# First batch of a cross-attention and feed-forward kernel: the second matrix mixed amid group 0's products, w_out pieces ordered behind w_in's, and a quarter of the products held back

## The chip, the cores and the metric

The kernel runs on one core of a Trainium2 chip. The metric is device microseconds of one launch. A change counts as faster or slower beyond 2%. Engines: PE (TensorE, matrix products), ACT (ScalarE), DVE (VectorE), SP (which issues most transfers).

## The reference

```python
# x: (8, 8, 512, 64), state: (8, 8, 32, 64); per batch and head
a     = softmax(scale * x @ state.T);  xread = a @ state
a2    = softmax(scale * state @ x.T);  sread = a2 @ x
rows  = concat([xread, sread])         # -> (8 * 544, 512)
h     = rows @ w_in                    # (512, 2048)
g     = h * erf(softplus(h))
out   = g @ w_out                      # (2048, 512)
```

Both weight matrices come as 64-bit floats and are turned into 32-bit on the chip, by bit operations.

## The kernel before

The weights come in sixteen pieces of 1 MB, eight of w_in and eight of w_out, two of each per group of 512 hidden columns. A piece lands in one of three raw buffers. Two instructions of ACT and three of DVE (L113, L114, L115 in the profile) convert it; then its raw buffer is free for the next transfer.

```python
raw = act.tile([P, 2 * shape[0] * i], U32, name="raw", bufs=3)
fetched.append(nc.sync.dma_start(out=raw..., in_=src.bitcast(U32)))
...
nc.scalar.activation(out=dst, in_=hi.bitcast(F32), func=ACTF.Copy, scale=2.0 ** -112)   # L111
nc.scalar.activation(out=lo, in_=lo, func=ACTF.Copy, scale=2.0 ** -29)                  # L112
nc.vector.tensor_scalar(d, d, 3, None, op0=ALU.logical_shift_left)                      # L113
nc.vector.tensor_tensor(d, d, lo, op=ALU.add)                                           # L114
nc.vector.scalar_tensor_tensor(out=d, in0=hi, scalar=0x80000000, in1=d, ...)            # L115
```

For each group of the first batch, `mixed` multiplies w_in by the state and copies the result out as the matrix m (L253 on PE, L255: one half copied by ACT, the other by DVE). `hidden` makes h in four banks (two in PSUM at a time; each is read by softplus on ACT, L272, and by a copy, L273). `finish` is one erf on ACT (L276) and one multiply on DVE (L277). `project` multiplies by w_out into four accumulators, here called blocks (L283).

```python
gT, hs, finish, banks = hidden(0, range(GF), 0, S, nc.scalar.copy)
...
at = finish()
acc = tiles(NC)
project(gT, 0, acc)
for g in range(1, NG):
    for j in range(2):
        behind(banks[j][:2] if g > 1 else at, weights_in, 2 * g + j)
    at, = mixed(0, g)
    for j in range(2):
        behind(at, weights_out, 2 * g + j)
    ...
    before, (gT, hs, finish, banks) = gT, hidden(0, range(GF * g, GF * g + GF), 0, S)
    at = finish()
    if g > 1:
        project(before, g - 1, acc)
```

`behind(marks, f, ...)` orders the instructions of f behind the marks in their engines' queues. The order in a queue is fixed when the program is built.

## Time and profile before

| what | before |
|---|---|
| time, median of 3 | 819.48 us |
| profiled run | 820.32 us, span 818.5 us |
| PE busy | 795.4 us, 97% of the span |
| PE waits between 36 and 82 us | 10.7 us in four waits |
| first w_out product | 38.82 us |
| third h bank of group 2 starts | 84.02 us |

The last two rows are milestones. The third bank of group 2 is where the stretch that the change touches ends; after it PE runs with hardly a gap (busy 726.1 of the 731.0 us from 84.02 to 815).

### The profile page before, as it was taken

To read this page: it belongs to the slowest core of one execution; us is meant where nothing else is said; L and a number is where in the kernel's file an instruction comes from. 1 tells how busy PE (TensorE), PEld (TensorE's weight loads), DVE (VectorE), ACT (ScalarE), POOL (GpSimd) and SP (SyncE) were. 2 spreads that over 40 slices of the span, in tenths; PEclk is the share of its full clock that TensorE was granted. 3 is DMA by queue.
4 is the path that set the end of the run, shared out by engine and by line. 5 is a ranking of instruction groups with operands and counts; after the bars stand their busy time and mean duration, and the time that the engine had idled before them with its cause. 6 is when DMAs were issued, how large, how long until landed. Compare 5 with 4: busy or idle time off the path is not lost.

```text
span 818.5 us, 10638 instructions
## 1 busy us (share of the span) xinstructions
PE 795.4 (97%) x4532; PEld 612.8 (75%) x4532; DVE 426.5 (52%) x622; ACT 370.0 (45%) x468; POOL 0.7 (0%) x6
## 2 busy tenths in 40 slices
PE   8887999999999999999999999999999999999997
PEld 7532444588888788878888788878887888888886
DVE  3748784458445554557453744555454745343431
ACT  5837554537333733345343733363334533333220
POOL 0000000000000000000000000000000000000000
PEclk9997999999999999999999999999999999999999
DMA  6636703201100030002000020000000000000000
GB/s 209 206 109 210 217 1 91 65 1 29 49 1 26 1 78 1 27 1 78 1 27 1 18 61 1 26 1 27 1 26 1 27 1 26 1 26 1 26 1 26
DMA packets 47414, 35.27 MB, mean 43 GB/s; under 512 B 36872, under 2 KB 36872, under 8 KB 47368
## 3 DMA queue, kind: packets, MB, share of 16 engines
q1 hardware_dynamic: 45256, 34.09, 13.4%
q10 hardware_dynamic: 2112, 0.52, 0.3%
q8 instruction: 35, 0.57, 0.3%
q14 instruction: 11, 0.09, 0.0%
HBM read 25.69 MB, written 8.91 MB: 42 GB/s over the span
## 4 chain that ended last, share of the span: by engine, by line
PE 86%; ACT 2%; DVE 1%; issue 1%
PE o L335 45%; PE h L270 28%; PE o L283 5%; PE at L253 4%; PE at L156 1%; PE at L214 1%; PE at L226 1%; PE at L179 1%; PE at L197 1%; ACT L272 1%; DVE s L277 1%; ACT s L272 0%; ACT xT L158 0%; ACT sc L170 0%; PE at L166 0%
## 5 line engine op out<-in xcount | busy, mean ns | idle before, releaser
L270 PE MATMUL h<-aT,m 128*128 128x256 f32 (+1 forms) x960 | 242.9, 400 | 3.9 <-DVE hs L273 3.1
L270 PEld LDWEIGHTS h<-aT,m 128*128 128x128 f32 x960 | 178.6, 191 | 68.1 <-issue 33.0
L273 DVE COPY hs<-h 128x512 f32<-128x512 f32 x132 | 90.7, 690 | 186.4 <-ACT s L272 186.2
L272 ACT ACTIVATE s<-h 128x512 f32<-128x512 f32 x136 | 80.3, 597 | 160.4 <-PE h L270 159.8
L277 DVE TENSOR_TENSOR s<-s,hs 128x2048 f32<-128x2048 f32 x34 | 77.9, 2292 | 76.0 <-ACT s L276 75.9
L335 PE MATMUL o<-w_out,s 128*128 128x256 f32 x480 | 114.9, 380 | 1.6 <-DVE s L277 1.6
L335 PE MATMUL o<-raw,hs 128*128 128x256 f32 x480 | 115.6, 380 | 0.0
L335 PE MATMUL o<-w_out,hs 128*128 128x256 f32 x480 | 113.4, 379 | 0.0
L335 PEld LDWEIGHTS o<-w_out,s 128*128 128x128 f32 x480 | 90.2, 190 | 14.3 <-DVE s L277 2.5
L335 PEld LDWEIGHTS o<-w_out,hs 128*128 128x128 f32 x480 | 91.1, 190 | 12.4
L335 PEld LDWEIGHTS o<-raw,hs 128*128 128x128 f32 x480 | 90.3, 190 | 12.4
L255 ACT COPY m<-at 128x512 f32<-128x512 f32 (+1 forms) x33 | 18.9, 573 | 165.4 <-PE at L253 165.3
L276 ACT ACTIVATE s<-s 128x2048 f32<-128x2048 f32 x34 | 64.9, 1910 | 0.4
L283 PE MATMUL o<-w_out,s 128*128 128x512 f32 x128 | 59.7, 607 | 1.8 <-DVE s L277 1.7
L335 PE MATMUL o<-raw,s 128*128 128x256 f32 x240 | 56.7, 379 | 0.0
L255 DVE COPY m<-at 128x512 f32<-128x512 f32 (+1 forms) x33 | 22.3, 675 | 60.0 <-PE at L253 60.0
L272 ACT ACT_TABLE_LOAD x40 | 51.3, 1283 | 0.7
L335 PEld LDWEIGHTS o<-raw,s 128*128 128x128 f32 x240 | 45.2, 190 | 5.9
L283 PEld LDWEIGHTS o<-w_out,s 128*128 128x128 f32 x128 | 23.4, 192 | 33.1 <-issue 29.2
L276 ACT ACT_TABLE_LOAD x34 | 43.6, 1283 | 0.6
L253 PE MATMUL at<-w_in,stT 64*32 64x512 f32 (+1 forms) x528 | 38.0, 602 | 5.6 <-DVE w_in L115 5.2
L346 ACT COPY m<-o 128x256 f32<-128x256 f32 x15 | 5.6, 373 | 57.3 <-PE o L335 57.3
(72 smaller groups left out, 584.8 us busy)
## 6 DMA issues: line engine op xcount, KB each, us to landing
raw<-in_moe_w_in_dram SPq DMA_DIRECT2D x8, 1024.0 KB, 5.3
raw<-in_moe_w_out_dram SPq DMA_DIRECT2D x8, 1024.0 KB, 4.9
out_dram<-ot SPq DMA_DIRECT2D x32, 256.0 KB, 2.4
x<-in_x_dram SPq DMA_DIRECT2D x60, 128.0 KB, 2.7
x<-in_x_dram ACTq DMA_DIRECT2D x4, 128.0 KB, 3.4
out_dram<-ot SPq DMA_DIRECT2D x8, 64.0 KB, 1.7
st<-in_state_dram SPq DMA_DIRECT2D x8, 56.0 KB, 4.4
st<-in_state_dram SPq DMA_DIRECT2D x2, 32.0 KB
```

The source lines that it names most:

```text
L156: nc.tensor.transpose(out=xp[:, P * c:P * c + P], in_=xt[:, c, 2 * i:2 * i + 2, :], identity=ident)
L179: on_pe = nc.tensor.transpose(out=s1[:, NI * c:NI * c + NI, :], in_=sc[:, e, P * c:P * c + P], identity=ident)
L197: nc.tensor.transpose(out=ps[:, P * c:P * c + P], in_=a[:, e, NI * c:NI * c + NI, :], identity=ident)
L253: nc.tensor.matmul(out=ps[e][q, :], lhsT=stT[b][r, q], rhs=w_in[r, fs, i, :], start=True, stop=True)
L255: return nc.scalar.copy(mg[:, 0], ps[0]), nc.vector.tensor_copy(mg[:, 1], ps[1])
L270: on_pe = nc.tensor.matmul(out=hp[:, n * j:n * j + n], lhsT=lhsT, rhs=rhs, start=(k == 0), stop=(k == len(ops) - 1))
L272: banks.append((nc.scalar.activation(out=s[:, i, :], in_=hp, func=ACTF.Softplus), copy(hs[:, i, :], hp), on_pe))
L273: copy(hs[:, i, :], hp), on_pe))
L276: return (nc.scalar.activation(out=s, in_=s, func=ACTF.Erf), nc.vector.tensor_tensor(s, s, hs, op=ALU.mult))
L277: nc.vector.tensor_tensor(s, s, hs, op=ALU.mult))
L283: nc.tensor.matmul(out=acc[r], lhsT=gT[:, i, P * r:P * r + P], rhs=w_out[:, GF * g + i, :], start=(g == 0 and i == 0), stop=(g == NG - 1 a ...
L335: nc.tensor.matmul(out=acc[bank][:, E2 * c:E2 * c + E2], lhsT=lhs[:, i, :], rhs=rhs[:, g, i, :], start=(first and i == 0 and c == 0), stop ...
```

## The change

Intent: (a) of group 0's four bank copies, two go to DVE, so that erf starts sooner. (b) The second matrix is mixed after two of the four blocks of group 0. (c) w_out piece 2 is converted directly behind the w_in pieces, in a stretch where ACT was idle, and w_in 4 directly behind w_out 3. (d) Block 3 is held back: three of its products run between the hidden banks of group 1, the last one after the third mixing.

```diff
-    gT, hs, finish, banks = hidden(0, range(GF), 0, S, nc.scalar.copy)
+    gT, hs, finish, banks = hidden(0, range(GF), 0, S,
+                                   [nc.scalar.copy] * 2 + [nc.vector.tensor_copy] * 2)
...
-    project(gT, 0, acc)
     for g in range(1, NG):
-        for j in range(2):
-            behind(banks[j][:2] if g > 1 else at, weights_in, 2 * g + j)
-        at, = mixed(0, g)
-        for j in range(2):
-            behind(at, weights_out, 2 * g + j)
+        if g == 1:
+            for j in range(2):
+                made = behind(at, weights_in, 2 + j)
+            project(gT, 0, acc, range(2))
+            at, = mixed(0, 1)
+            behind([made], weights_out, 2)
+            made = behind(at, weights_out, 3)
+            project(gT, 0, acc, range(2, 3))
+        else:
+            if g == 2:
+                behind([made], weights_in, 4)
+                behind(banks[1][:2], weights_in, 5)
+                project(gT_, 0, acc, range(3, 4), range(GF - 1))
+            else:
+                for j in range(2):
+                    behind(banks[j][:2], weights_in, 2 * g + j)
+            at, = mixed(0, g)
+            if g == 2:
+                project(gT_, 0, acc, range(3, 4), range(GF - 1, GF))
+            for j in range(2):
+                behind(at, weights_out, 2 * g + j)
```

(The converting function returns its last instruction, and `project` takes ranges of blocks and products.)

More of the change, by code (lines that the diff above doesn't have):

```diff
@@ L114, in weight @@
         nc.vector.tensor_tensor(d, d, lo, op=ALU.add)
-        nc.vector.scalar_tensor_tensor(out=d, in0=hi, scalar=0x80000000, in1=d,
-                                       op0=ALU.bitwise_and, op1=ALU.bitwise_or)
+        return nc.vector.scalar_tensor_tensor(out=d, in0=hi, scalar=0x80000000, in1=d,
+                                              op0=ALU.bitwise_and, op1=ALU.bitwise_or)
     gw = GF * P
     def weights_in(j):
-        weight(w_in[:, j],
-               moe_w_in[:, 2 * P * j:2 * P * j + 2 * P].rearrange("(k p) f -> p k f", p=P),
-               (NK, 2 * P))
+        return weight(w_in[:, j],
+                      moe_w_in[:, 2 * P * j:2 * P * j + 2 * P].rearrange("(k p) f -> p k f", p=P),
+                      (NK, 2 * P))
     def weights_out(j):
-        weight(w_out[:, 2 * j:2 * j + 2, :],
-               moe_w_out[2 * P * j:2 * P * j + 2 * P].rearrange("(t p) e -> p t e", p=P),
-               (2, d_model))
+        return weight(w_out[:, 2 * j:2 * j + 2, :],
+                      moe_w_out[2 * P * j:2 * P * j + 2 * P].rearrange("(t p) e -> p t e", p=P),
+                      (2, d_model))
     spare = ps_o.tile([P, d_model], F32, name="o3")
@@ L255, in mixed_part, with hidden @@
         return nc.scalar.copy(mg[:, 0], ps[0]), nc.vector.tensor_copy(mg[:, 1], ps[1])
-    def hidden(b, fts, t0, n, copy=nc.vector.tensor_copy):
+    def hidden(b, fts, t0, n, copies=(nc.vector.tensor_copy,) * 4):
         hs = act.tile([P, 4, S], F32, name="hs")
@@ L272, in hidden @@
             banks.append((nc.scalar.activation(out=s[:, i, :], in_=hp, func=ACTF.Softplus),
-                          copy(hs[:, i, :], hp), on_pe))
+                          copies[i](hs[:, i, :], hp), on_pe))
         def finish():
@@ L278, in hidden, with project @@
         return s, hs, finish, banks
-    def project(gT, g, acc):
-        for r in range(NC):
-            for i in range(GF):
+    def project(gT, g, acc, rs=range(NC), ts=range(GF)):
+        for r in rs:
+            for i in ts:
                 nc.tensor.matmul(out=acc[r], lhsT=gT[:, i, P * r:P * r + P],
@@ L430 @@
             states(1)
-        before, (gT, hs, finish, banks) = gT, hidden(0, range(GF * g, GF * g + GF), 0, S)
+        gT_, (gT, hs, finish, banks) = gT, hidden(0, range(GF * g, GF * g + GF), 0, S)
         at = finish()
@@ L435 @@
         if g > 1:
-            project(before, g - 1, acc)
+            project(gT_, g - 1, acc)
     last = combine_w()
```

## The prediction

> **What bounds the kernel now.** I read the page first: busy time by engine, the 40 slices, and the chain that ended last.
>
> ```profile
> PE 795.4 (97%) x4532; PEld 612.8 (75%) x4532; DVE 426.5 (52%) x622; ACT 370.0 (45%) x468; POOL 0.7 (0%) x6
> ...
> PE   8887999999999999999999999999999999999997
> ...
> PEclk9997999999999999999999999999999999999999
> ...
> PE 86%; ACT 2%; DVE 1%; issue 1%
> ```
>
> The chain is matrix products (PE) for 86% of the span. The only slices with a visible hole are the first four (20.5 us each), and in the fourth the clock falls too. After that PE is the bound, so a microsecond saved early should arrive unchanged at the end. The change touches only the first batch, so I went to the list of waits of PE between 36 and 82 us.
>
> ```profile
> PE at L253 <- DVE w_in L115: 5.2, 1, 5.2
> PE h L270 <- DVE hs L273: 3.1, 1, 3.1
> PE o L283 <- DVE s L277: 1.7, 1, 1.7
> PE h L270 <- ACT m L255: 0.7, 1, 0.7
> ```
>
> Columns: who waited for whom, total us, times, longest. Then PE alone in order of time over the same stretch (start, length, what, idle before):
>
> ```profile
> 52.75 1.09 PE L253 MATMUL at<-w_in,stT 64*32 64x512 f32 x16
> 54.57 3.70 PE L270 MATMUL h<-aT,m 128*128 128x512 f32 x8 [0.73 <-ACT m L255]
> 61.39 5.36 PE L270 MATMUL h<-aT,m 128*128 128x512 f32 x8 [3.12 <-DVE hs L273]
> 71.91 1.96 PE L253 MATMUL at<-w_in,stT 64*32 64x512 f32 x16 [5.15 <-DVE w_in L115]
> ```
>
> Eight records took 3.70 us in the second row and 5.36 in the third; sixteen took 1.09, then 1.96. The table of one-microsecond stretches says why (the clock is the third number from the right):
>
> ```profile
> 61.00:62.00 1.00, 0.61 (x1) 0.50 (x2) 1.00 (x2) 1.00 (x2) 0.00 (x0) 0.68 0.89 188
> 64.00:65.00 1.00, 1.00 (x3) 0.46 (x2) 1.00 (x1) 0.00 (x0) 0.00 (x0) 0.62 0.95 356
> 71.00:72.00 1.00, 0.10 (x8) 0.13 (x16) 1.00 (x2) 0.63 (x1) 0.00 (x0) 0.80 0.80 328
> 78.00:79.00 1.00, 1.00 (x3) 0.32 (x2) 1.00 (x2) 0.98 (x2) 0.00 (x0) 0.79 0.00 0
> ```
>
> The clock fell to half at about 61.36, rose at 64.75, fell at 71.6, rose at 78.4. So two waits cost 8.3 us, and each cost more afterwards through a slow clock. ACT in order of time shows the cause of both:
>
> ```profile
> 54.41 1.13 ACT L111 ACTIVATE w_out<-raw 128x1024 f32<-128x1024 f32 x1
> ...
> 57.52 1.17 ACT L112 ACTIVATE raw<-raw 128x1024 uint32<-128x1024 uint32 x1
> 58.70 1.28 ACT L272 ACT_TABLE_LOAD   x1
> 60.00 1.08 ACT L272 ACTIVATE s<-h 128x512 f32<-128x512 f32 x2
> ```
>
> Between 40.6 and 53.9 ACT did nothing; at 54.4 it began converting two w_out pieces, just when PE filled its two h banks, and only then evicted them.
>
> [...] 61.36 to 64.75 is 3.4 us, 71.6 to 78.4 is two of them. And the fall at 61.36 came after only 3.1 us of complete idleness. [...] A 128x512 product stands as two records, start to start 0.43 us: 0.857 us per product. [...] the reload before softplus is a fixed 1.28 us. [...] here a piece lands a median 5.2 us after issue (4.8 at the least), and that is what I use.
>
> **The change, part by part.** Arithmetic, bytes and number of products stay. Order moves. I compared the instruction order of the two builds and placed the new order in time with durations of the trace. Steps start to start: conversion on ACT 1.03 per half; on DVE L113 0.60 (0.81 if the next reads it), L114 and L115 1.14 (1.26 if the next reads it); bank copy or softplus 0.6.
>
> (a) Bank copies 2 and 3 of group 0 go from ACT to DVE. ACT has two copies between its softpluses; now the second softplus waits for its product (ends 31.75) and ends 32.40, so the table load starts at 32.41 instead of 33.23: 0.83 earlier. DVE is free: copies at 32.5 and 33.1, the delayed L115 ends at 34.9, before the multiply, due at 35.64 (36.47 before). First w_out product 38.82 -> 37.99. Gain 0.83.
>
> (b) Second matrix amid the products. PE does two of four blocks (8 x 0.857 = 6.86): 44.85. w_in pieces 2 and 3 are converted at 43.99 (44.83 less the 0.83), so mixing runs 45.1 to 46.2 without a wait. Block 2 (3.43) covers the copy of m, until 49.55: the 0.73 wait goes. Four products of hidden fill both h banks until 52.98; three of the kept four run until 55.55.
>
> (c) w_out pieces behind w_in's. Piece 2, issued about 35.0, lands near 41, and is converted by 47.2, in ACT's old hole. Piece 3 needs a raw buffer (three exist), free when DVE finishes the first w_in piece at 42.85; issued 42.9, lands about 47.8. ACT converts it 47.8 to 50.0, then w_in 4 (issued 44.05, landed near 50.1) until 52.3; table load until 53.6, softplus of both banks until 54.8. DVE: piece 3 until 52.5, w_in 4 52.4 to 55.7, bank copies done 56.3 and 56.9. So PE waits 55.55 to 56.40: 0.85 in place of 3.12, and does four products until 59.83.
>
> (d) w_in 5 takes the buffer of w_out 2: issued 47.25, landed by 53, converted on DVE 56.8 to 60.1. PE mixes at 60.27: a wait of 0.45 in place of 5.15, until 61.36; the last kept product runs to 62.15.
>
> (e) A new wait. The copy of m on ACT stands behind softplus of bank 3 (60.5), table load (61.8) and erf (63.7), so it ends at 64.2, and PE has nothing else: 2.1 us idle. Then four products to 67.7, five of group 1 to 72.0, and the third h bank starts.
>
> That last point was at 84.02 before, is now 71.97: 12.05 us earlier. Check by sums: before, from the end of block 3 at 52.5 to 84.02 is 31.5 us; its work is two mixings (2.04), 12 hidden products (10.28) and five others (4.29), 16.6 us. So 14.9 were lost: 9.0 in three waits, the rest by slow clock and changeovers. After, 0.85 + 0.45 + 2.1 + about 0.5 of changeovers, 3.9, remain. 14.9 - 3.9 + 0.83 = 11.8, near the 12.05.
>
> Do the later pieces follow? w_in 6 is issued near 60, w_in 7 near 69.7 and lands by 75. Its conversion ends near 82, and PE wants it at 84.8. w_out 4 and 5 lie between, converted by 72.5, and are wanted at the same time. So nothing eats the gain, by a margin of about 3 us.
>
> **The rivals.** First, the 2.1 us hole of (e) chills the clock. The stretch around it has mixing (small tiles) and one product in it; a mostly idle window sufficed at 58 to 61.4. For it: [...] mixing may count little, as the clock stayed half through 71.9 to 75. Against: 37.1 to 38.8 was idle 1.7 us with no fall, and here the worst window still holds some 1.3 us of work. It would cost one window, about 1.7 us, or two, 3.4: 809 to 811. I give it 15 to 20%. Second, the conversions are the bound: with PE's waits small, the path from 47.8 runs through landing, ACT and DVE. Each microsecond that piece 3 or w_in 4 lands late moves everything after it. For it: both are in flight at once, as in 45 to 51 us before, and share the engines. It makes 808 to 809. Third, the gain is given back later because weights arrive no earlier (waits at third mixing): the margin above speaks against it; it would leave 5 to 8 us of gain, 811 to 814. Fourth, better than thought: earlier landings or no wait for erf, 805.5.
>
> **Range and chances.** 819.5 less 12 gives 807.5. Low 805.5: the 2.1 and the two small waits halved. High 811: a chilled clock, or late pieces. Faster by over 2% needs 16.4 us, but all that was lost is 14.9, and (a) adds 0.83: 15.7. That nearly rules it out: 1%. Slower would need a new stall of over 28 us: 1%.
>
> **What would show each step.** (a) first w_out product near 38.0. (b) mixing at about 45, with no wait at its hidden products. (c) a wait of 0.5 to 2 us at the third h bank, on DVE's copy. (d) under 1 us before the mixing of the third matrix. (e) about 2 us before the next hidden products, on ACT's m. Clock at full rate from 55 to 80. Third h bank of group 2 near 72 instead of 84, and the same distance to the end of the kernel. Wrong: a clock of half after 62, the wait at the third bank above 3 us, or a wait on w_in in the fourth group.

The steps and lengths are from the profile of the kernel before: records of a 128x512 product 0.43 us apart, two per product; the table load 1.283 us (each of the 40 at L272, so "fixed"); landings of 4.8 to 9.7 us, in the median 5.2 (`--tile raw`, 0 to 110 us). The half clock of "one window, about 1.7 us" is the 3.41 us from 61.36 to 64.77. That two pieces in flight share the engines is read off the stretch from 45 to 51 us: the 16 DMA engines were busy for 93% of it and moved 2.07 MB, 345 GB/s.

## The result, and the profile after

The changed kernel took 810.41 us (median of four, 808.74 to 812.89); the kernel before, beside it, 819.72. The ratio is 0.9886, with an interval of 0.9855 to 0.9916. That is 9.3 us less, inside the predicted range of 805.5 to 811, and 2.9 us more than the predicted 807.5. By the 2% rule above the verdict is "same", for this kernel and for all twelve of the experiments; the intervals show that all but `copies_only` are below the kernel before all the same.

The profiled run was the slowest of the four, 812.89 us (above the predicted range). Three lines of its page:

```profile
PE 792.5 (98%) x4532; PEld 611.7 (75%) x4532; DVE 427.9 (53%) x624; ACT 369.3 (46%) x466; POOL 0.7 (0%) x6
...
PEclk9999999999999999999999999999999999999999
...
PE 88%; ACT 3%; DVE 1%; DMA 1%; issue 1%; SPq 0%
```

The 7 in the fourth slice of the clock row is gone. In the chain that ended last, DMA now has 1%: a transfer has come onto the path, where the chain before showed none (nor does that of `again`, below). PE's waits between 36 and 82 us:

```profile
PE h L270 <- DVE hs L273: 2.5, 1, 2.5
PE h L270 <- ACT m L255: 2.0, 1, 2.0
PE o L283 <- DVE s L277: 0.9, 1, 0.9
PE at L253 <- DVE w_in L115: 0.2, 1, 0.2
```

The sum fell from 10.7 to 5.6 us. The wait on the w_in conversion went from 5.2 to 0.2. A new one of 2.0 on ACT's copy of m is what step (e) of the prediction named, and is called the hole from here on. PE in order of time (start, length, what, idle before):

```profile
58.76 3.70 PE L270 MATMUL h<-aT,m 128*128 128x512 f32 x8 [2.55 <-DVE hs L273]
62.71 1.09 PE L253 MATMUL at<-w_in,stT 64*32 64x512 f32 x16 [0.25 <-DVE w_in L115]
66.85 5.40 PE L270 MATMUL h<-aT,m 128*128 128x512 f32 x8 [1.98 <-ACT m L255]
```

The first and the third row are eight records of the same kind, once 3.70 and once 5.40 us. The one-microsecond stretches show the clock (third number from the right):

```profile
67.00:68.00 1.00, 1.00 (x2) 0.48 (x3) 1.00 (x1) 1.00 (x2) 0.00 (x0) 0.59 0.15 55
...
70.00:71.00 1.00, 1.00 (x3) 0.53 (x2) 1.00 (x2) 0.98 (x2) 0.00 (x0) 0.70 0.00 0
```

It fell to half near 67.2 and rose near 70.6, 3.41 us later, which cost 1.7. Before, it was at half from 61.36 to 64.77 and from 71.60 to 78.43, three times as long. The chain of waits tells where the 2.55 came from (start, length, what):

```profile
44.52 8.87 DMA raw<-in_moe_w_in_dram
...
54.44 1.16 ACT raw L112
...
55.62 1.24 DVE w_in L114
...
56.88 1.22 DVE w_in L115
58.11 0.61 DVE hs L273
```

Piece w_in 4 was 8.9 us on its way; its conversion stands ahead of the bank copies on DVE, so the bank copies waited for it.

The third h bank of group 2 starts at 76.37 instead of 84.02: 7.65 us earlier, and the span is 7.7 us shorter (810.8 against 818.5). So the gain is whole at that milestone and nothing after it gives any back. That holds in the other traces too: from the milestone to the end it is 734.4 to 734.8 us in both kernels and in those runs whose PE order from there on is theirs. (In `w_out_late`, `m_on_dve` and `early_m_dve` one product fewer of 0.86 us lies ahead of the milestone and one more behind it: 735.3 us.)

The table places the changed kernel's two profiles (the second is from the experiment `again`) against the prediction, counted from the first w_out product, which sits at 37.8 to 39.5 us depending on how the head of the run (its first 30 us or so) went.

| from the first w_out product, us | predicted | first profile | second profile |
|---|---|---|---|
| third bank of group 1 | 18.41 | 20.34 | 18.38 |
| third mixing | 22.28 | 24.29 | 22.29 |
| hidden products of group 2 | 26.26 | 28.43 | 26.47 |
| third bank of group 2 | 33.98 | 37.95 | 35.99 |

(Predicted: 56.40, 60.27, 64.25 and 71.97 less 37.99. Before, the last row was 84.02 - 38.82 = 45.20.)

### The profile page after: what moved, and what is told of

Same layout as the page of the kernel before. It is cut to its first block, busy times and chain, and to the rows that moved or that the text cites. A ratio compares the mean times of both kernels' runs of the same rounds, so it can differ in the third digit from the quotient of the medians.

```text
span 810.8 us, 10642 instructions
## 1 busy us (share of the span) xinstructions
PE 792.5 (98%) x4532; PEld 611.7 (75%) x4532; DVE 427.9 (53%) x624; ACT 369.3 (46%) x466; POOL 0.7 (0%) x6
## 4 chain that ended last, share of the span: by engine, by line
PE 88%; ACT 3%; DVE 1%; DMA 1%; issue 1%; SPq 0%
PE o L335 45%; PE h L270 29%; PE o L283 5%; PE at L253 4%; PE at L156 1%; DMA raw<-in_moe_w_in_dram 1%; PE at L214 1%; PE at L226 1%; PE at L179 1%; PE at L197 1%; ACT L272 1%; ACT s L276 0%; ACT s L272 0%; ACT L276 0%; ACT xT L158 0%
## 5 line engine op out<-in xcount | busy, mean ns | idle before, releaser
L272 ACT ACTIVATE s<-h 128x512 f32<-128x512 f32 x136 | 80.2, 597 | 160.5 <-PE h L270 159.9
```

What stands on the lines that cost most here:

```text
L272: banks.append((nc.scalar.activation(out=s[:, i, :], in_=hp, func=ACTF.Softplus), copies[i](hs[:, i, :], hp), on_pe))
```

## The experiments

Twelve kernels, each timed over five rounds beside the kernel before. All but the first undo or isolate a part of the change, or take away one suspected cost. All gave correct results. Runs of one call share a chip and the runs of the kernel before.

### again

The changed kernel unaltered.

> The changed kernel unaltered, for its own spread and a second profile. Theory A (the chain runs from the landing of weight piece w_in 4 through ACT, DVE and the third h bank to the erf and the copy of m): the landing was late because the next piece was in flight beside it, so it is late again: wait at the third bank 2 to 3 us, a hole of about 2 us before the third matrix's hidden products, time near 810. Rival B (the late landing was chance): landing about 6 us after issue, wait near 0.9, time near 808. The clock falls to half after the hole in some profiles and not in others[...].

Measured: 810.91 us (809.01 to 812.55), ratio 0.989 (0.9872 to 0.9907). Its PE rows at the same three places:

```profile
56.57 3.70 PE L270 MATMUL h<-aT,m 128*128 128x512 f32 x8 [0.60 <-DVE hs L273]
60.48 1.09 PE L253 MATMUL at<-w_in,stT 64*32 64x512 f32 x16 [0.20 <-DVE w_in L115]
64.66 5.40 PE L270 MATMUL h<-aT,m 128*128 128x512 f32 x8 [2.03 <-ACT m L255]
```

The wait at the third bank was 0.60, and w_in 4 was converted 6.3 us after its issue (44.27 to 50.55). The same two transfers were under way, so the late landing of the first profile was chance (its cause stays open): rival B was right on the mechanism, theory A wrong. But the time did not fall to B's 808: the clock fell to half in the hole here too. Over the nine runs of the two sets, the mean clock was 0.999 or 1.0 in two (808.74 and 809.01 us) and 0.998 or less in seven (810.26 us or more in each, on average 811.2). A stretch of 3.41 us at half clock lowers the mean by 3.41 x 0.5 / 810 = 0.002. The mean alone proves no fall in the hole, for it also counts the end of the run, where PE is done and the clock drops (the kernel before is at half from 815.7 us to its last instruction at 818.5, with PE idle; the profile of `hole_warm` is at half from 806.1 us on, falls nowhere else, and has 0.999). But with the gap in the times, 1.25 us, it makes a fall in the hole likely in those seven, and three of the four profiles of this order with an empty hole show it.

### copies_only

```diff
-    gT, hs, finish, banks = hidden(0, range(GF), 0, S, nc.scalar.copy)
+    gT, hs, finish, banks = hidden(0, range(GF), 0, S,
+                                   [nc.scalar.copy] * 2 + [nc.vector.tensor_copy] * 2)
```

(on the kernel before)

> The kernel before with part (a) alone: bank copies 2 and 3 of group 0 on DVE. If the erf's early start is worth its full length: first w_out product 0.8 us earlier, the rest shifted with it, time 0.8 us under before. Rival: the w_out conversion on DVE, now 1.3 us later, frees its raw buffer later and gives it back: same time as before.

Measured: 819.69 us, ratio 1.0002 (0.9988 to 1.0016). In the trace, from the start of the 24 warming products to the first w_out product it is 6.40 us (32.65 to 39.05), against 7.22 before (31.60 to 38.82): the 0.82 is there locally. At the third bank of group 2 only 0.4 of it is left (52.03 us from the warming products, against 52.42). In the time it does not show; 0.8 us is 0.1%, and lies within the interval.

### copies_back

The same edit reversed, on the changed kernel.

> The changed kernel with part (a) taken back (all four copies on ACT). Theory A: the erf starts 0.8 us later, the transfers that wait for the DVE conversions behind it are issued 0.8 us later: time 0.8 us above the changed kernel. Rival: the path from 44 us on starts with transfers, whose landing absorbs it: within 0.3 us.

Measured: 809.89 us (809.19 to 810.94), ratio 0.988 (0.9866 to 0.9894): no slower than the changed kernel. Locally it lost the same: 7.24 us to the first w_out product. From the two, part (a) is worth at most about 1 us, and the times cannot tell 0.8 from nothing. The profile is worth more for another reason. Its hole is as long as in `again`, 2.04 us, and the eight records took 3.70:

```profile
64.82 3.70 PE L270 MATMUL h<-aT,m 128*128 128x512 f32 x8 [2.04 <-ACT m L255]
```

The same hole with and without a fall: its length alone did not decide whether the clock fell. The traces show what went with the falls. All changes of the clock in one trace lie whole multiples of 3.41 us apart (in the kernel before the stretches between them are 54.61, 3.41, 6.83, 6.83 and 737.28 us, so 16, 1, 2, 2 and 216 times 3.413), on a grid that lies elsewhere in each run (the falls in the hole came at 67.18 in the first profile, 64.96 in `again` and 64.6 in `w_in5_later`); so I counted PE's busy time in each window of the grid. First the window that ended in the fall of the changed kernel, then the one of `copies_back` that holds most of the hole (window, length, PE busy; the clock is third from the right):

```profile
63.77:67.18 3.41, 1.43 (x8) 0.56 (x4) 1.57 (x3) 3.40 (x4) 0.00 (x0) 1.00 0.89 298
...
63.37:66.79 3.42, 1.97 (x5) 1.01 (x6) 2.46 (x2) 3.42 (x5) 0.00 (x0) 1.00 0.50 195
```

In the first the hole lies in one window, of which PE was busy 42%; in the second a border at 63.37 divides it, and the windows held 77% and 58%. Between 36 and 82 us of all fourteen traces, each of the eleven windows that ended in a fall held at most 1.54 us of PE work (45%, `w_in5_later`), and each full-speed window that did not held at least 1.59 (47%, the changed kernel from 56.94 us). The clock came back after a window at half clock of which PE was busy 93% or more, and stayed down after 87% or less; six of the eleven falls lasted one window, four lasted two and one three (`copies_only`, 69.3 to 79.5). The busy times are modelled, so these figures are rough, and they are those of these fourteen traces.

With no fall, the third bank of group 2 stands 34.20 us behind the first w_out product, against 33.98 predicted; but without part (a) that product itself comes 0.84 us later. In `hole_warm`, next, which has part (a) and no fall, it is 34.48.

### hole_warm

```diff
             hp = ps_h.tile([P, S], F32, name="h")
+            if i == 0 and b == 0 and fts[0] == 2 * GF:
+                for _ in range(8):
+                    nc.tensor.matmul(out=hp[:, 0:P], lhsT=ident, rhs=ident, start=True, stop=True)
```

> The changed kernel with 8 idle 128x128 products with the identity put into the hole, in the free h bank that the next product overwrites. They do no work and take no engine that anything waits for. Theory A: the hole stays (the hidden products still start at the copy of m), but the clock does not fall, and the eight records take 3.7 us instead of 5.4: about 1.7 us under the changed kernel in runs where that one's clock fell, and less spread. Rival: the fall has another cause, and the records take 5.4 again.

Measured: 809.09 us (808.53 to 809.90), ratio 0.9863 (0.9843 to 0.9882). The mean clock was 0.999 or 1.0 in all four runs (in 3 of the 13 runs of the changed kernel in `again`, `w_in5_later` and the result).

```profile
63.66 1.95 PE L269 MATMUL h<-ident 128*128 128x128 f32 x16
65.82 3.70 PE L273 MATMUL h<-aT,m 128*128 128x512 f32 x8 [0.21 <-ACT m L255]
```

Idle work of 1.95 us in the hole (here 16 records, two per product) and the next records take 3.70. The hole stays as long; only the clock is kept. Against the two unaltered kernels that is 1.3 to 1.8 us less, and against `w_in5_later` (below, in effect unaltered, same chip) 1.25. The cause of the slow records after this hole is thereby shown: it is PE's idleness in it (3.70 us with the idle products, 5.32 to 5.40 in three of the four profiles without). The times alone would not show it, for the two intervals overlap.

### m_on_dve

```diff
-        return nc.scalar.copy(mg[:, 0], ps[0]), nc.vector.tensor_copy(mg[:, 1], ps[1])
+        copy = nc.vector.tensor_copy if (b, g) == (0, 2) else nc.scalar.copy
+        return copy(mg[:, 0], ps[0]), nc.vector.tensor_copy(mg[:, 1], ps[1])
```

> The changed kernel with both copies of m of the third matrix on DVE, so that none stands behind softplus, table load and erf on ACT. Theory A: the hole shrinks from 2.0 to about 0.6 us and the clock stays: 1.4 plus 1.7 us, so about 3 us under a changed kernel whose clock fell, near 807. Rival: the DVE copy delays the multiply and the conversions behind it, and the wait returns one group later: same time.

Measured: 808.60 us (808.48 to 809.00), ratio 0.9857 (0.9838 to 0.9875).

```profile
62.62 3.70 PE L271 MATMUL h<-aT,m 128*128 128x512 f32 x8
67.84 3.70 PE L284 MATMUL o<-w_out,s 128*128 128x512 f32 x8 [1.52 <-DVE s L278]
```

The hole is gone and the clock stayed up, as theory A has it. But a wait of 1.52 us came after, on DVE's multiply of group 1, which is the rival's point. So the saving was about the clock's 1.7, not 3 us. By the medians, and with a narrow spread, this is the best of all kernels run: 1.7 us under `w_in5_later`, and 1.4% under the kernel before. Its lead of 0.5 us on `hole_warm` and `early_m_dve` is not clear of noise.

### none_kept

```diff
-            project(gT, 0, acc, range(2, 3))
+            project(gT, 0, acc, range(2, 4))
```

(and the two held-back calls removed)

> The changed kernel with no products kept back: block 3 of group 0 runs whole before the hidden products of group 1. Theory A (PE is not the bound between 46 and 67 us): the third h bank starts where it did (near 58.8), with a wait of about 2 us in place of 2.5; the hole before the third matrix's hidden products grows from 2.0 to about 2.9 us, they start where they did, and the clock falls more surely; time within 1 us of the changed kernel. Rival D (the kept quarter hides waits): up to 3.4 us slower.

Measured: 810.78 us, ratio 0.9883 (0.9859 to 0.9906): as the changed kernel. Its PE rows:

```profile
62.98 1.09 PE L253 MATMUL at<-w_in,stT 64*32 64x512 f32 x16 [2.34 <-DVE w_in L115]
65.02 5.29 PE L270 MATMUL h<-aT,m 128*128 128x512 f32 x8 [0.95 <-ACT m L255]
```

There is no wait at the third bank at all; the waiting stands before the third mixing instead. I had the places of the waits wrong (2 us at the bank and 2.9 in the hole were expected). But the sum is about the same (3.3 us, in `again` 2.8), because PE only moves its idle time about: the hidden products of group 2 start 26.54 us after the first w_out product, in `again` 26.47. Part (d) is worth nothing here that the times show.

### w_out_late

```diff
-            behind([made], weights_out, 2)
+            behind(at, weights_out, 2)
```

> The changed kernel with w_out piece 2 ordered behind the copy of m again, as before (part (c) taken back). Theory A (transfers and conversions in sum set the pace, whichever comes first): piece w_in 5 is issued some 4 us later, so w_in 4 lands alone, near 50 us, the wait at the third bank falls under 1 us, and the third mixing starts within 1 us of where it was; time within 1 us of the changed kernel. Rival C (filling ACT's hole is the gain): 3 to 5 us slower than the changed kernel.

Measured: 812.16 us (811.46 to 812.69), ratio 0.9906 (0.9893 to 0.992): 1.3 to 1.8 us slower than the changed kernel, more than the 1 us that theory A allowed and less than rival C's 3 to 5 (the intervals of the two ratios overlap, so that this rests on the medians and on the trace). The wait at the third bank is gone, but piece w_in 5 came later and the whole wait stands before the third mixing:

```profile
63.53 1.96 PE L253 MATMUL at<-w_in,stT 64*32 64x512 f32 x16 [3.30 <-DVE w_in L115]
```

The sixteen records take 1.96: after a wait of 3.3 us in one piece the clock was down, and it stayed at half from 63.44 to 70.24 in this profile, two windows. The first w_out product is 37.16 us before the third bank of group 2, 1.2 more than in `again`; with one product fewer in between, like for like 2.0 more.

### only_amid

The kernel before with part (b), built from the changed kernel by taking (a), (d) and the order of w_out 2 back. One order of (c) stayed: w_in 4 stands behind w_out 3. So this is not (b) alone, as the expectation has it.

```diff
+            project(gT, 0, acc, range(2))
+            at, = mixed(0, 1)
+            behind(at, weights_out, 2)
+            made = behind(at, weights_out, 3)
+            project(gT, 0, acc, range(2, 4))
```

> The kernel before with part (b) alone: second matrix mixed after two of the four blocks of group 0; copies on ACT, w_out pieces behind the copy of m, nothing kept. Theory A': the loss of before was ACT idle until the copy of m at 54 us, with both w_out conversions behind it; mixing at 46 brings that copy, and so the conversions, 7 us forward all by itself. Third mixing near 63.5 as with the w_out pieces late; time within 1.5 us of that run, 811 to 813, most of the gain. Rival (the parts add up): about a third of the gain, 816.

Measured: 814.59 us (813.30 to 815.07), ratio 0.9925 (0.9912 to 0.9937). Two of PE's rows:

```profile
59.56 3.70 PE L270 MATMUL h<-aT,m 128*128 128x512 f32 x8 [1.53 <-DVE hs L273]
...
67.65 6.77 PE L270 MATMUL h<-aT,m 128*128 128x512 f32 x8 [2.37 <-ACT m L255]
```

### not_amid

Parts (a) and (c) without (b) and (d): PE's order is that of before.

```diff
+            project(gT, 0, acc)
+            behind([made], weights_out, 2)
+            at, = mixed(0, 1)
+            made = behind(at, weights_out, 3)
```

> Parts (a) and (c) without (b) and without kept products: PE's order as before, w_out piece 2 behind the w_in pieces on ACT and DVE. Theory A': this fills ACT's idle time by the other way, so most of the gain stays too: third bank near 59, third mixing near 65, time 811 to 813. Rival (the parts add up, and the mixing amid the products is the main one): 815 or more.

Measured: 815.03 us (814.37 to 815.99), ratio 0.9936 (0.9922 to 0.995). Two of PE's rows:

```profile
59.46 3.70 PE L270 MATMUL h<-aT,m 128*128 128x512 f32 x8 [1.51 <-DVE hs L273]
67.21 1.96 PE L253 MATMUL at<-w_in,stT 64*32 64x512 f32 x16 [4.05 <-DVE w_in L115]
```

Theory A' missed twice: each half gave less than it said. `only_amid` lies between theory and rival; `not_amid` is where the rival had it (815 or more), though mixing amid is then hardly the main part. Mixing amid took off 0.75% and filling ACT's idle time 0.64%; together that would be 1.39%, and the whole change took off 1.1 to 1.14%. So the halves are nearer to adding up than to replacing each other. Where they overlap is not shown: both kernels have w_in 4 behind w_out 3, which alone could be what is counted twice, and no run took that order away. The traces show where each falls short. In `only_amid` the clock was at half for two windows behind the hole, 67.04 to 73.84 (6.77 us for the eight records). In `not_amid` the copy of m on ACT stood behind the conversion of w_in 4, and w_in 5 was ready only at 67.1.

### w_in5_later

```diff
+                act.tile([P, 2 * GF * P * 2], U32, name="raw", bufs=3)
                 behind(banks[1][:2], weights_in, 5)
```

> The changed kernel with an unused raw buffer taken between w_in 4 and w_in 5, so that w_in 5's transfer waits for the conversion of w_out 3 (issue near 53 instead of 48 us). Theory A (w_in 5 in flight beside it makes w_in 4 late): w_in 4 lands within 6.5 us of its issue, the wait at the third bank falls under 1 us; w_in 5 lands near 58.5, so the third mixing waits 2 to 3 us, and the time stays within 1 us. Rival B: w_in 4 lands 8 to 9 us after its issue here too, and the time rises by 3 us.

Measured: 810.34 us, ratio 0.9873 (0.9853 to 0.9894). The experiment did not do what it was for: a buffer that is taken and never used is not held, every engine's order is that of the changed kernel, and w_in 5 was issued at 47.3 us as there. So it says nothing of its question, and counts as another repeat: w_in 4 converted 7.2 us after issue, wait at the third bank 0.87, eight records after the hole in 5.32 us.

### early_piece

```diff
-        raw = act.tile([P, 2 * shape[0] * i], U32, name="raw", bufs=3)
+        if spare_hs:     # w_out piece 3
+            raw = act.tile([P, 4, S], F32, name="hs")...bitcast(U32)
+        else:
+            raw = act.tile([P, 2 * shape[0] * i], U32, name="raw", bufs=3)
```

> The changed kernel with w_out piece 3 landing in the free half of the hs buffers, so that its transfer is issued near 27 us and each later piece gets its raw buffer one conversion earlier (w_in 4 near 43, w_in 5 near 44.5). Theory A: the landing of w_in 4 is off the path, the wait at the third bank falls from 2.5 to under 1 us, the third mixing starts near 59 instead of 62.7; the hole of about 2 us stays. About 3 us under the changed kernel, near 807. Rival: ACT and DVE, with the same conversions to do, are the bound, and the wait stays above 2 us: same time.

Measured: 809.38 us (809.15 to 811.50), ratio 0.9871 (0.9849 to 0.9893).

```profile
57.10 3.60 PE L273 MATMUL h<-aT,m 128*128 128x512 f32 x8
...
65.08 3.70 PE L273 MATMUL h<-aT,m 128*128 128x512 f32 x8 [2.25 <-ACT m L258]
```

The trace does what was expected: no wait at the third bank, third mixing 21.21 us behind the first w_out product (22.29 in `again`), hole left. The gain over the changed kernel is 1.0 to 1.5 us by the medians and not clear of noise. The 3 us expected were measured against the one profile with the late landing, and that was no typical run.

### early_m_dve

Both edits.

> Both: w_out piece 3 early in the hs buffer, and both copies of the third matrix's m on DVE. Theory A: the two waits are in series, so the gains add: wait at the third bank under 1 us, hole under 1 us, clock at full rate throughout; 5 to 6 us under the changed kernel, near 804.5, against 807 for either alone.

Measured: 809.05 us (808.86 to 809.28), ratio 0.9857 (0.9837 to 0.9877). The gains did not add. Its third bank of group 2 stands 33.53 us behind the first w_out product, with m on DVE alone 33.28; in both the built order puts one product fewer (0.86 us) ahead of it, so like for like they are 34.4 and 34.1, and the early piece alone is 33.44. Two rows:

```profile
62.86 3.70 PE L274 MATMUL h<-aT,m 128*128 128x512 f32 x8 [1.41 <-DVE m L259]
68.09 3.70 PE L287 MATMUL o<-w_out,s 128*128 128x512 f32 x8 [1.52 <-DVE s L281]
```

With the copies of m on DVE, the builder put one w_out conversion of group 2 and half of the other ahead of the last softplus on ACT; that half waited 1.11 us for its transfer, and the softplus with it; on DVE the copies of m and the multiply stood behind its bank copy, and PE waited twice.

## Why the prediction was right, point by point

The range held for the median, and the order of work with its waits was right. The clock was not: "clock at full rate from 55 to 80" failed, and "a clock of half after 62", one of the three signs that the prediction named for being wrong, came true. The centre was 2.9 us too low, and the range held through its upper end, which had been set for this very case ("a chilled clock, or late pieces"); three of the nine unaltered runs lie above it (811.05, 812.55, 812.89).

- (a), first w_out product 0.83 us earlier: 0.82 in the trace, counted from the warming products. Its worth at the end is not shown; `copies_only` and `copies_back` leave it between nothing and about 1 us.
- (b), second mixing near 45 without a wait at its hidden products: 45.49, no wait.
- (c), a wait of 0.85 us in place of 3.12 at the third bank: 0.50 to 0.87 in five of the six profiles with this order (the changed kernel twice, `copies_back`, `hole_warm`, `m_on_dve` and `w_in5_later`), and 2.55 in one, where piece w_in 4 came 8.9 us after issue instead of the roughly 6 that I took. That is the second rival, in one run, and above the 0.5 to 2 us that the prediction's own check allowed.
- (d), under 1 us before the third mixing: 0.20 to 0.25 in the same six.
- (e), a hole of 2.1 us: 1.98 to 2.04.
- The third bank of group 2 near 72 us instead of 84: missed, 76.37 and 74.18 in the two profiles.
- From that milestone to the end nothing is given back: shown, 7.65 us there and 7.7 at the end.

What was off is one term and one starting point. The term is the clock after the hole. I gave its fall 15 to 20%, and counted nothing for it in the centre. It fell in three of the four profiles of this order with an empty hole (not in `copies_back`; nor in `early_piece`, with a hole of 2.25), and costs 1.7 us (5.40 against 3.70): the whole difference between the predicted 33.98 and the 35.99 of `again`, but for 0.3. `hole_warm`, with idle products for 1.95 us of the hole and the next records in 3.70, shows that it was the idleness that did it. The argument that "the worst window still holds some 1.3 us of work" had the amount right and its effect wrong: 1.3 of 3.41 us is 38%, and each of the eleven falls seen here came after a window with 1.54 us (45%) or less. The profile before could not tell this: its falls came after windows of 9% and 0%, and the idle 1.7 us at 37.1 to 38.8, which the prediction held against a fall, lay in a window of 60%. The starting point is that the working was done against a profile whose own run took 820.32 us, and the 12.05 was then taken off the median of 819.48, 0.84 us lower. 1.7 and 0.84 make 2.5 of the 2.9; late landings in some runs may be the rest, which I have not shown.

Two slips of the working did no harm. It says that it uses 5.2 us for a landing, but takes 6.05 for w_in 4 (44.05 to 50.1), 4.9 for w_out 3 and 5.75 for w_in 5; the first was the nearer to what came, 6.3 to 7.2. And halving the three waits of its low end takes off 1.7 us, which gives 805.8 and not 805.5.

The bound of 15.7 us on the possible gain held: no kernel run here took off more than 1.43%.

## What to carry to other kernels

Where PE waited here on a chain of transfer, conversion and bank copy, moving PE's own instructions about only moved its waits (holding products back was worth nothing: 810.78 us without, 810.41 and 810.91 with), unless it started the chain earlier; that is what paid, and it took both mixing sooner and converting sooner, each giving about 0.6 to 0.7 of the gain in the builds tried. Follow each engine's fixed order to the next wait: here a hole of 2 us on PE also cost 1.7 us of clock afterwards in three of four profiles, and filling it with idle products got that back (3.70 us for the next records instead of 5.40). Gains taken off one chain did not add where the next wait stood right behind it (`early_m_dve`, 809.05 us, against 809.38 and 808.60 for its two parts), and a profile that is a slow run of its kernel is a poor base for subtracting.

## What else the traces show of landings and the clock

- From issue to use: the same 1 MB piece (w_in 4) at the same place of the same order was used 6.3 to 7.2 us after issue in six profiles, each with ACT waiting for it, and 8.9 in one; in the first profile after, pieces elsewhere landed in 4.6 to 9.2. The spread matters as much as the median of that profile, 5.4.
- The clock fell in the head of a run as well. In two of fourteen profiles it was at half for about 3.4 us, in `copies_only` from 7.84 to 11.24 us and in `early_piece` from 8.96 to 12.36. Between 6 and 8 us PE was busy for 0.79 and 0.82 us in these two, for 0.93 to 1.57 in the other twelve, which show no such fall. The first w_out products of the two came at 39.05 and 39.47 instead of 37.8 to 38.5 in nine of the other twelve. The other three: the kernel before (38.82) and `only_amid` (39.39) lack part (a); for `hole_warm` (39.17) the cause is not shown.
